# Seven half products in place of eight for w_out in some pair stages, sums of x kept in DRAM, half of each value tile copied on chip

## Chip, cores and metric

The kernel runs on one core of a Trainium2 chip. The metric is the device time of one execution in microseconds (us); lower is better. Engines: PE multiplies matrices, DVE and ACT (and POOL, GpSimd) work on elements, SP issues the DMA transfers.

## What is computed

The reference applies attention with a local window and 32 global tokens per sequence, then two feed-forward layers, all in fp32:

```
s_ll = where(|i - j| <= 32, q_l @ k_l.T * scale, -1e9)      # local rows: window
a_l  = softmax([q_l @ k_g.T * scale, s_ll]);  out_l = a_l @ [v_g, v_l]
out_g = softmax(q_g @ [k_g, k_l].T * scale) @ [v_g, v_l]     # 32 global rows
x = reshape(out, (2304, 512))                               # 4 sequences x 576 tokens
x = max(x @ w_in, 0)**2 @ w_out                             # moe:  512 -> 2048 -> 512
x = max(x @ w2_in, 0)**2 @ w2_out                           # moe2: the same shape
```

## The kernel before

Tokens stand in columns, features in partitions. The 2304 tokens are five blocks: block 0 (384 columns, with the global tokens), pair A (blocks 1 and 2, 512 columns each) and pair B (blocks 3 and 4, 384 each). Every fp32 operand is split into a high and a low part (`whi`, `wlo`; `xh`, `xl`; `gh`, `gl`), and a product is three passes on PE: high x high, high x low, low x high (L584 to L586).

Each layer has eight stages of 256 hidden features, that is two chunks of w_in and two of w_out (128 x 512 each, "weights"). The first stage of the first layer ("begin") runs among the attention, block by block. The other 15 run afterwards, each over block 0, pair A and pair B in the order that `CFG['order']` names. A weight arrives as 64-bit numbers in `wraw` (one buffer) by SP's queue, is turned into fp32 in `wt` by one ACT or DVE and four DVE instructions (L505 to L516) and split into a slot of `whi`/`wlo` (9 slots).

For w_in, a pair is multiplied by the scheme of Strassen and Winograd: seven half products instead of eight. It takes two weight slots with sums of the two chunks (`sums`, L530) and three sums of x per pair (`tsums`, L750), which are split once per layer and lie in SBUF (`tAh`, `tAl`, `tBh`, `tBl`). The half products collect in PSUM and in staging tiles `r` (L720). Then `activate` squares the positive part and splits it into `gh` and `gl`, and `second` multiplies by w_out: per block four output tiles `d`, each from two chunks, six passes. `finish` adds each into `y` (L642).

Attention works on 32 pairs of heads: keys and queries `kq`, values `v` (eight slots of 128 x 130: the window of each group of 32 queries, so most values come twice from DRAM), scores (L332), softmax, transposes (L355), values (L369), transposes back into x (L387). PE also runs warm-up matmuls on zeros (L805) wherever nothing else is ready.

Nothing is ordered by hand: `Plan` records all operations with priorities, costs and dependences, and `Plan.order` plays them in its own clock and writes the program in the order that results. On the chip each engine, SP's queue too, keeps to its order and waits where an operand is late.

Of the kernel before, what the change touches and what calls it, by code (L numbers as in the profile page):

```python
# [21 lines left out]
UNITS = 8  # L22
NI = UNITS * H
WIN = 224
KEYS = 128
VW = 2 * (D + 1)
KW = 384
# [9 lines left out]
CFG = {'warm': 32,  # L37
 'sg': 'A',
 'tl': 'D',
 'EARLY': 8,  # L40
 'ev': 'AAAA',
 'yc': 'ADAD',
 'wl': 'DD',
 'gl': 'D',
 'xh': 'AA',
 'glob': [13.66, 40.71, 52.94, 62.9],
 'w0': 0.0,
 'w1': 2.444332206519449,
 'halves': [1],
 'moe': [-728.245, 2019.27, 252.018, 414.177, 727.924, -1738.197],  # L50
 'step': [0.3996, 0.0017, 4.1427, 0.0632, 2.0927, 0.4659],
 'NK': 4,
 'wa': 'DADAAAA',
 'lid': -2.391,
 'lmk': -70.51,
 'lead': 6.47,
 'vlead': 1.531,
 'NM': 2,
 'NS': 5,
 'NV': 2,  # L60
 'NR': 9,
# [31 lines left out]
class Plan:  # L93
# [36 lines left out]
    def order(self):  # L130
# [8 lines left out]
        while len(done) < len(self.ops):  # L139
# [67 lines left out]
def pe_r(n, m=128):  # L207
    return max(n + 32.5, 2 * m + 6) / 2400
# [3 lines left out]
def kernel(ctx: ExitStack, tc: tile.TileContext, kl, vl, gk, gv, win, wout, msk, idn, out):  # L212
# [64 lines left out]
    kg = tiles(ap_, "kg", 2, [128, 1152 + S])  # L277
    gmx = ap_.tile([128, 2, 2], F32, name="gmx")
    gsm = ap_.tile([128, 2], F32, name="gsm")
    masks = ap_.tile([128, 3, KEYS], F32, name="masks")  # L280
    ident = ap_.tile([128, 128], F32, name="ident")
    warm = ap_.tile([128, 128], F32, name="warm")
    zeros = warm[:, 0:1].to_broadcast([128, 272])
    late_opened, tt_ = [], {}

    def open_late():
        if not late_opened:
# [11 lines left out]
    cnt = {"S": 0, "PT": 0, "O": 0, "h": 0, "Y": 0, "r": 0, "x": 0}  # L299
# [6 lines left out]
    def load(prio, out_, in_, nbytes, reads, writes):  # L306
        add("SP", 0.475, prio, lambda: nc.sync.dma_start(out=out_, in_=in_), reads, writes, tail=nbytes / 380e3)


    def pair(j, prio):  # L310
# [11 lines left out]
        load(prio - lead, kq[kb], kl[j], 327680, A, (K,))  # L322
        load(prio - CFG["vlead"], vt[vb], vl[j], 128 * 32 * VW, A, (V,))
        sk = [take("S", CFG["S"]) for _ in range(2)]

        def scores():
            for t in range(2):
                for g in range(4):
                    c, w = KW + 128 * t + 32 * g, 160 * t + 32 * g
                    for e in range(2):  # L330
                        r = slice(64 * e, 64 * e + 64)
                        nc.tensor.matmul(out=bank[sk[e]][32 * g:32 * g + 32, t * KEYS:(t + 1) * KEYS],  # L332
                                         lhsT=kq[kb][r, c:c + 32], rhs=kq[kb][r, w:w + KEYS], start=True, stop=True)

        add("PE", 0.503, P(), scores, A + (K,), tuple(sk), mode="S")
        for e in range(2):
            s = sk[e]
            for t in range(2):
                qt = (u % 2) * 2 + t
                mi = 0 if qt == 0 else (2 if qt == 3 else 1)  # L340
                k = 2 * e + t
                add("DVE", 0.21, P(), lambda t=t, mi=mi, k=k, s=s: nc.vector.tensor_tensor_reduce(
                    out=st[sb][:, k, :], in0=bank[s][:, t * KEYS:(t + 1) * KEYS], in1=masks[:, mi, :],
# [29 lines left out]
        add("PE", 0.5, P(), pv, A + every + (V,), (ok,), mode="V")  # L373
# [29 lines left out]
    def glob(bb, prio):  # L403
# [14 lines left out]
        for g in range(2):  # L418
            load(prio - 2.9 + 0.05 * g, V[g][:, 0:1280], gv[2 * bb + g], 655360, A, (GV[g],))
# [537 lines left out]
```

## Time and profile before

| | before |
|---|---|
| time, median of 3 runs | 833.05 us (832.01 to 834.45) |
| profiled execution: time, span | 832.85 us, 831.1 us |
| PE, DVE, ACT, POOL busy | 817.9, 675.5, 432.1, 0.2 us |
| mean granted PE clock | 0.999 |
| DMA, mean over the span | 92 GB/s |

The span reaches from the first to the last instruction; 1.75 us of the execution lie around it. Busy times count an engine's time once, also where instructions overlap.

### The profile page before, as it was taken

The numbers are of one execution on the slowest core, as the hardware profiler recorded it, in microseconds if no ns is written. First come the engines' busy times: TensorE is split into PE (matmuls) and PEld (weight loads), VectorE is DVE, ScalarE is ACT, GpSimd is POOL, SyncE is SP. The second block draws the span as 40 slices with busy tenths as digits, with TensorE's granted clock in tenths as the row PEclk, the third lists the DMA queues.
The fourth block names the chain that finished last, engine by engine and source line by source line (L and its number), as shares of the span: only waits on it lengthen the run. The fifth ranks groups of instructions, "written<-read, shape, count | busy, mean of one in ns | idle before, by whom it ended". The sixth has DMA issues, their size and how long they took to land.

```text
span 831.1 us, 16130 instructions
## 1 busy us (share of the span) xinstructions
PE 817.9 (98%) x6504; PEld 728.2 (88%) x6504; DVE 675.5 (81%) x1580; ACT 432.1 (52%) x934; POOL 0.2 (0%) x4
## 2 busy tenths in 40 slices
PE   9899999999999999999999999999999999999998
PEld 7676767899898998899898998899898989989997
DVE  4779788997887788878889998878887879688654
ACT  5886967653445334535356666535444444445341
POOL 0000000000000000000000000000000000000000
PEclk9999999999999999999999999999999999999999
DMA  9899874101111012102020111102020102020023
GB/s 348 309 371 315 307 244 171 50 2 51 52 52 51 26 54 74 51 26 73 30 76 1 34 52 68 51 26 77 26 77 26 55 22 77 26 77 26 26 76 140
DMA packets 23978, 76.79 MB, mean 92 GB/s; under 512 B 2656, under 2 KB 4448, under 8 KB 23904
## 3 DMA queue, kind: packets, MB, share of 16 engines
q1 hardware_dynamic: 23904, 75.77, 25.6%
q8 instruction: 51, 0.84, 0.4%
q14 instruction: 23, 0.19, 0.1%
HBM read 71.30 MB, written 4.46 MB: 91 GB/s over the span
## 4 chain that ended last, share of the span: by engine, by line
PE 91%; DMA 4%; DVE 3%; ACT 2%; issue 1%; ACTq 0%; DVEq 0%
PE O L585 7%; PE O L586 7%; PE O L584 7%; PE h L584 7%; PE h L586 7%; PE h L585 7%; PE S L586 6%; PE S L585 6%; PE S L584 6%; PE Y L584 4%; PE Y L586 4%; PE Y L585 4%; PE PT L586 4%; PE PT L584 4%; PE PT L585 4%; DMA v<-vl 2%
## 5 line engine op out<-in xcount | busy, mean ns | idle before, releaser
L243 DVE TENSOR_TENSOR gl<-r,gh 128x384 fp32r<-128x384 f32 (+2 forms) x162 | 97.5, 603 | 52.0 <-ACT r L613 43.5
L584 PE MATMUL O<-gh,whi 128*128 128x384 f32 (+1 forms) x304 | 108.2, 356 | 0.0
L586 PE MATMUL O<-gh,wlo 128*128 128x384 f32 (+1 forms) x304 | 108.2, 356 | 0.0
L585 PE MATMUL O<-gl,whi 128*128 128x384 f32 (+1 forms) x304 | 108.2, 356 | 0.0
L539 ACT ACTIVATE whi<-wt 128x512 fp32r<-128x512 f32 x94 | 58.7, 626 | 79.0 <-DVE wt L516 63.6
L642 DVE TENSOR_TENSOR y<-y,O 128x384 f32<-128x384 f32 (+1 forms) x140 | 82.0, 602 | 11.0 <-PE O L586 10.8
L584 PE MATMUL h<-xh,whi 128*128 128x384 f32 (+2 forms) x210 | 75.8, 361 | 0.0
L243 DVE TENSOR_TENSOR wlo<-wt,whi 128x512 fp32r<-128x512 f32 x94 | 64.4, 686 | 12.3 <-ACT whi L539 12.3
L585 PE MATMUL h<-xl,whi 128*128 128x384 f32 (+2 forms) x210 | 73.5, 350 | 0.7 <-DVE xl L399 0.7
L586 PE MATMUL h<-xh,wlo 128*128 128x384 f32 (+2 forms) x210 | 73.4, 350 | 0.0
L584 PE MATMUL Y<-gh,whi 128*128 128x384 f32 (+2 forms) x192 | 69.9, 364 | 0.5 <-DVE y L231 0.5
L585 PE MATMUL S<-xl,whi 128*128 128x384 f32 (+1 forms) x198 | 69.9, 353 | 0.0
L586 PE MATMUL S<-xh,wlo 128*128 128x384 f32 (+1 forms) x198 | 69.9, 353 | 0.0
L584 PE MATMUL S<-xh,whi 128*128 128x384 f32 (+1 forms) x198 | 69.7, 352 | 0.0
L586 PE MATMUL Y<-gh,wlo 128*128 128x384 f32 (+2 forms) x192 | 67.5, 352 | 0.1
L585 PE MATMUL Y<-gl,whi 128*128 128x384 f32 (+2 forms) x192 | 67.5, 351 | 0.0
L585 PEld LDWEIGHTS O<-gl,whi 128*128 128x128 f32 x304 | 57.1, 188 | 4.8
L586 PEld LDWEIGHTS O<-gh,wlo 128*128 128x128 f32 x304 | 57.1, 188 | 4.7
L584 PEld LDWEIGHTS O<-gh,whi 128*128 128x128 f32 x304 | 57.1, 188 | 4.7
L606 ACT ACTIVATE gh<-r 128x512 fp32r<-128x512 f32 (+1 forms) x60 | 34.7, 578 | 47.0 <-DVE r L604 46.9
L613 ACT ACTIVATE r<-r 128x384 f32<-128x384 f32 (+2 forms) x102 | 56.6, 555 | 3.1
L610 ACT ACTIVATE gh<-r 128x384 fp32r<-128x384 f32 (+2 forms) x102 | 56.0, 549 | 2.3 <-PE O L586 0.5
(125 smaller groups left out, 1846.6 us busy)
## 6 DMA issues: line engine op xcount, KB each, us to landing
v<-vl SPq DMA_DIRECT2D x32, 520.0 KB, 5.3
wraw<-win SPq DMA_DIRECT2D x32, 512.0 KB, 3.2
wraw<-wout SPq DMA_DIRECT2D x32, 512.0 KB, 3.3
kq<-kl SPq DMA_DIRECT2D x32, 320.0 KB, 5.5
y<-gv SPq DMA_DIRECT2D x8, 640.0 KB, 7.5
kg<-gk SPq DMA_DIRECT2D x8, 576.0 KB, 8.2
out<-y SPq DMA_DIRECT2D x12, 192.0 KB, 1.9
out<-y SPq DMA_DIRECT2D x8, 256.0 KB, 2.9
```

The source lines that it names most:

```text
L243: add("DVE", dve(n), prio, lambda: nc.vector.tensor_tensor(out=get(out_), in0=get(a), in1=get(b), op=ALU.subtract), reads, writes, lock=True)
L539: nc.scalar.activation(out=whi[slot], in_=tf, func=AF.Copy)
L584: nc.tensor.matmul(out=out_, lhsT=hi, rhs=xhi, start=start, stop=False, skip_group_check=again)
L585: nc.tensor.matmul(out=out_, lhsT=hi, rhs=xlo, start=False, stop=False, skip_group_check=again)
L586: nc.tensor.matmul(out=out_, lhsT=lo, rhs=xhi, start=False, stop=stop, skip_group_check=again)
L606: add("Activation", act(nb) + 0.04, P(), lambda: nc.scalar.activation(out=a, in_=r, func=AF.Copy), (R,), GH)
L610: add("Activation", act(nb) + 0.04, P(), lambda: nc.scalar.activation(out=a, in_=r, func=AF.Square), (R,), GH)
L613: add("Activation", act(nb) + 0.04, P(), lambda: nc.scalar.activation(out=r, in_=r, func=AF.Square), (), (R,))
L642: add("DVE", dve(nb), P(), lambda: nc.vector.tensor_tensor(out=yd, in0=yd, in1=o, op=ALU.add), (yk[d],), (Y,))
```

## The change

Three parts, and a new table of numbers (`CFG`) that sets priorities, buffers and engines.

1. **w_out in seven half products.** `CFG['so']` names the pairs of each stage that use it. `back` multiplies there seven half products of two output tiles, with two more weight slots that hold sums of the w_out chunks, and with differences of the squared activations (`mix`, L904), in place of the two calls of `second`. Each half product belongs to one or two places of `y` and is added there (`deliver`, L697), so there are 12 or 14 additions per pair in place of 8. Squares stay in `r` and are split by `op`.
2. **Sums of x in DRAM.** They are written to `saved` when they are made and read back before each pair's products into a ring of six tiles `tr`.
3. **Half of the value tiles copied on chip.** DMA brings four of the eight slots, POOL copies the rest.

The table changes, among others: 11 weight slots, 13 staging tiles, 3 value tiles, 4 slots in place of 8 before the attention's memory is free, 11 warm-up matmuls, one low part of a weight in four on POOL (`wl`), squares on ACT (`gs`) but one in four (`gf`), evictions on ACT.

```diff
-CFG = {'warm': 32,
+CFG = {'warm': 11,
...
+ 'EARLY': 4,
+ 'vc': 'PP',
+ 'ev': 'A',
+ 'yc': 'A',
+ 'wl': 'DPDD',
...
- 'NR': 9,
+ 'NV': 3,
+ 'NR': 13,
...
+ 'NSLOT': 11,
+ 'NG': 4,
+ 'NTR': 6,
...
+ 'tm': 'RRRR',
+ 'so': ['', 'AB', 'A', 'A', 'AB', '', '', 'A', 'AB', 'A', 'AB', 'B', 'AB', 'AB', 'A'],
+ 'wp': [-242.15, -537.45],
...
+ 'gf': 'ADAA',
+ 'gs': 'A',
...
+    drm = ctx.enter_context(tc.tile_pool(name="drm", bufs=1, space=bass.MemoryType.DRAM))
+    saved = {(g, n, i): drm.tile([128, 2, NB[b]], F32, name=f"td{g}{n}{i}")
+             for g, (b, _) in PAIRS.items() for n in (2, 3, 4) for i in range(2)}
...
-            for g, (b, _) in PAIRS.items():
-                for n in (2, 3, 4):
-                    tt_[g, n] = [lp.tile([128, 2, NB[b]], F32R, name=f"t{g}{k}{n}") for k in "hl"]
...
+            for j in range(NTR):
+                tring.append(lp.tile([128, 2, 512], F32R, name=f"tr{j}"))
...
-        load(prio - lead, kq[kb], kl[j], 327680, A, (K,))
-        load(prio - CFG["vlead"], vt[vb], vl[j], 128 * 32 * VW, A, (V,))
+        load(prio - lead, kq[kb], kl[j], 512 * (KW + 256), A, (K,))
+        load(prio - CFG["vlead"], vt[vb][:, 0:4 * VW], vl[j], 128 * 16 * VW, A, (V, ("v2", vb)))
+        for p0, n, to, src in ((0, 128, 4, 0), (0, 32, 4, 1), (0, 64, 6, 1), (64, 64, 6, 0)):
+            rows = slice(p0, p0 + n)
+            copy("vc", prio - CFG["vlead"] + 1e-3, vt[vb][rows, to * VW:(to + 2) * VW], vt[vb][rows, src * VW:(src + 2) * VW],
+                 2 * VW, A + (V,), (("v2", vb),))
...
-                (half(t0, 1), half(t0, 1), half(t1, 1), ALU.subtract, (T1,), T0)):
+                (half(t0, 1), half(t0, 1), half(t1, 1), ALU.subtract, (T1,), T0)) if kind == "in" else (
+                (half(t1, 1), half(t0, 1), half(t1, 1), ALU.add, (T0,), T1),
+                (half(t0, 1), half(t0, 0), half(t0, 1), ALU.subtract, (), T0),
+                (half(t0, 0), half(t1, 1), half(t0, 0), ALU.subtract, (T1,), T0),
+                (half(t1, 0), half(t1, 0), half(t0, 0), ALU.subtract, (T0,), T1))):
...
+            add("DVE", dve(nb), P(), lambda: nc.vector.tensor_tensor(out=yd, in0=yd, in1=o, op=ALU.add), (k,), (Y,))
...
+        activate(P, f, nb, hp, hk, half)
...
+        def t(n):
+            got = []
+            for i in range(2):
+                if (g, n, i) in direct:
+                    r, R = direct.pop((g, n, i))
+                else:
+                    r, R = granule()
+                    lr, lw = late_keys(R)
+
...
+                    load(P(), dst, saved[g, n, i], 1024 * nb, (("td", g, n, i, 0), ("td", g, n, i, 1)) + lr, (R,) + lw)
+                got.append((lambda r=r: tring[r][:, 0, 0:nb], lambda r=r: tring[r][:, 1, 0:nb], R))
...
+        if fork:
+            copy("sf", P(), A, B, nb, (kb,), (ka,), psum=True)
+        else:
+            keep(0)
+        product(kc, C, sa, 0, x(b1, 0), True)
         product(kb, B, sa, 2, t(2), False)
         keep(1)
...
+        product(ka, A, f0, 2, x(b0, 2), not fork)
+        if fork:
+            square(P, nb, A, ka, s[0], G[0])
+        else:
+            plus(0, ka, A)
+            square(P, nb, s[0], G[0], s[0], G[0])
...
+        add("Activation", act(nb) + 0.04, P(), hi, (R,) + lr, GH + lw)
+        minus("gl", P(), l, r, lambda: a().bitcast(F32), nb, (R,) + GH, GL)
+        return f
...
+    def back(W, g, P, sG, stages):
...
+        (r11, r12, r22, r21), (R11, R12, R22, R21) = sG
+        (o0, o1), (p1, p0) = W["out"], W["osum"]
+        banks = [take("Y", CFG["Y"] + CFG["PT"] + CFG["O"]) for _ in range(4)]
...
+        def product(two, slot, h, X, start, ys):
+            a, l, K = X
+            for d in range(2):
+                o = bank[two[d]][:, 0:nb]
+                add("PE", c3, P(), lambda o=o, d=d: three(
+                    o, wv(whi, slot)[:, 2 * h + d, :], wv(wlo, slot)[:, 2 * h + d, :], a(), l(), start, True, not start),
+                    (("w", slot),) + K, (two[d],))
+                for b, k in ys:
+                    n = seen[b, k + d] = seen.get((b, k + d), 0) + 1
+                    last = 1 if (b, k) == (b0, 2) or (forked and (b, k) == (b0, 0)) else 2
+                    deliver(P, b, k + d, two[d], stages, None, stages[1] and n == 1, stages[2] and n == last)
...
+        X, K = banks[0:2], banks[2:4]
+        B21, B11 = opd(r21, R21), opd(r11, R11)
+        forked = pick("sx") == "A" and min(wide.get(k, 0) for k in X) >= nb
...
+        if forked:
+            product(K, o0, 0, B11, True, ())
+            for d in range(2):
+                add("Activation", act(nb), P(), lambda d=d: nc.scalar.activation(
+                    out=bank[X[d]][:, 0:nb], in_=bank[K[d]][:, 0:nb], func=AF.Copy), (K[d],), (X[d],))
+            product(X, o1, 0, B21, False, ((b0, 0),))
+        else:
+            product(X, o1, 0, B21, True, ((b0, 0),))
+            product(K, o0, 0, B11, True, ((b0, 0),))
+        mix(r12, r12, r11, (R11,), R12)
+        product(X, p1, 1, opd(r12, R12), True, ((b1, 2),))
+        B22 = opd(r22, R22)
+        mix(r22, r22, r12, (R12,), R22)
+        product(K, p0, 0, opd(r22, R22), False, ((b1, 0),))
+        product(X, p1, 0, B22, False, ((b1, 0),))
+        mix(r11, r22, r11, (R22,), R11)
+        product(K, p0, 1, opd(r11, R11), False, ((b1, 2),))
+        mix(r21, r21, r22, (R22,), R21)
+        product(K, o1, 1, opd(r21, R21), False, ((b0, 2),))
...
+            if n == 1:
+                hi_, lo_, K = lambda: xh[b1][:, i, :], lambda: xl[b1][:, i, :], (("x", b1, i),) * 2
+            elif ring:
+                r, R = granule()
+                direct[g, n, i] = r, R
+                lr, lw = late_keys(R)
+                hi_, lo_, K = lambda: tring[r][:, 0, 0:nb], lambda: tring[r][:, 1, 0:nb], (R, R)
+            else:
+                (v, V), (w, X) = staging(), staging()
+                hi_, lo_, K = lambda: v[:, 0:nb].bitcast(F32R), lambda: w[:, 0:nb].bitcast(F32R), (V, X)
...
+            if n > 1:
+                for e, f in enumerate((hi_, lo_)):
+                    load(P(), saved[g, n, i][:, e, :], lambda f=f: f().bitcast(F32), 512 * nb, (K[e],), (("td", g, n, i, e),))
```

PE, in the second stage after the attention, w_out on 512 columns (`Y`, `PT`, `O` are PSUM banks; equal names with other numbers are other buffers). Before, at the end of pair A: each bank gets two chunks (slots 105/113 and 100/108).

```order
L584 MATMUL PT_147<-gh_79,whi_105 128x512
L585 MATMUL PT_147<-gl_83,whi_105 128x512
L586 MATMUL PT_147<-gh_79,wlo_113 128x512
L584 MATMUL PT_147<-gh_80,whi_100 128x512
L585 MATMUL PT_147<-gl_84,whi_100 128x512
L586 MATMUL PT_147<-gh_80,wlo_108 128x512
L584 MATMUL O_148<-gh_79,whi_105 128x512
L585 MATMUL O_148<-gl_83,whi_105 128x512
L586 MATMUL O_148<-gh_79,wlo_113 128x512
L584 MATMUL O_148<-gh_80,whi_100 128x512
L585 MATMUL O_148<-gl_84,whi_100 128x512
L586 MATMUL O_148<-gh_80,wlo_108 128x512
```

Now, in the middle of pair A: slot 2756/2757 and slot 2750/2751 hold sums of the two w_out chunks; half products go to two banks each.

```order
L636 MATMUL Y_163<-gh_80,whi_2756 128x512
L637 MATMUL Y_163<-gl_84,whi_2756 128x512
L638 MATMUL Y_163<-gh_80,wlo_2757 128x512
L636 MATMUL PT_166<-gh_80,whi_2756 128x512
L637 MATMUL PT_166<-gl_84,whi_2756 128x512
L638 MATMUL PT_166<-gh_80,wlo_2757 128x512
L636 MATMUL O_167<-gh_82,whi_2750 128x512
L637 MATMUL O_167<-gl_86,whi_2750 128x512
L638 MATMUL O_167<-gh_82,wlo_2751 128x512
L636 MATMUL O_168<-gh_82,whi_2750 128x512
L637 MATMUL O_168<-gl_86,whi_2750 128x512
L638 MATMUL O_168<-gh_82,wlo_2751 128x512
```

What moved: sixteen bank visits of three passes for a pair become fourteen, and the visits wait for the differences of the activations in turn.

DVE, the same stage, pair B. Before: half products into `r`, squares (L604), low parts (`gl`), with a weight's steps among them.

```order
L720 TENSOR_TENSOR r_92<-r_92,S_146 128x384
L512 TENSOR_SCALAR wt_97<-wt_97 128x512
L604 SCALAR_TENSOR_TENSOR r_92<-r_92 128x384
L514 SCALAR_TENSOR_TENSOR wt_97<-wraw_96,wt_97 128x512
L243 TENSOR_TENSOR gl_84<-r_92,gh_80 128x384
L516 SCALAR_TENSOR_TENSOR wt_97<-wraw_96,wt_97 128x512
L720 TENSOR_TENSOR r_91<-r_91,S_146 128x384
L243 TENSOR_TENSOR gl_86<-r_93,gh_82 128x384
L604 SCALAR_TENSOR_TENSOR r_91<-r_91 128x384
L243 TENSOR_TENSOR wlo_114<-wt_97,whi_106 128x512
L243 TENSOR_TENSOR gl_83<-r_91,gh_79 128x384
L642 TENSOR_TENSOR y_77<-y_77,Y_144 128x384
```

Now: no squares on DVE here, the differences (L904) and additions into y between them.

```order
L264 TENSOR_TENSOR wlo_2761<-wt_102,whi_2760 128x512
L264 TENSOR_TENSOR gl_86<-r_94,gh_82 128x384
L820 TENSOR_TENSOR r_95<-r_95,S_164 128x384
L264 TENSOR_TENSOR gl_84<-r_96,gh_80 128x384
L264 TENSOR_TENSOR gl_85<-r_97,gh_81 128x384
L904 TENSOR_TENSOR r_95<-r_95,r_94 128x384
L904 TENSOR_TENSOR r_96<-r_96,r_95 128x384
L904 TENSOR_TENSOR r_94<-r_96,r_94 128x384
L697 TENSOR_TENSOR y_77<-y_77,Y_163 128x384
L697 TENSOR_TENSOR y_77<-y_77,PT_166 128x384
L264 TENSOR_TENSOR gl_83<-r_95,gh_79 128x384
L264 TENSOR_TENSOR gl_85<-r_96,gh_81 128x384
```

What moved: differences, their low parts and the additions into `y` stand in one chain with the next half products.

SP's queue, some stages later. Before, it holds only weights:

```order
L307 DMA wraw_96<-win 128x1024
L307 DMA wraw_96<-wout 128x1024 x2
L307 DMA wraw_96<-win 128x1024 x2
L307 DMA wraw_96<-wout 128x1024 x2
L307 DMA wraw_96<-win 128x1024 x2
L307 DMA wraw_96<-wout 128x1024 x2
```

Now the reads of sums (`tdA`, `tdB`) stand among the weights:

```order
L348 DMA tr_2769<-tdA_154 128x1024
L348 DMA tr_2764<-tdA_149 128x1024
L348 DMA wraw_100<-win 128x1024
L348 DMA tr_2765<-tdA_150 128x1024
L348 DMA tr_2766<-tdA_151 128x1024
L348 DMA wraw_100<-wout 128x1024
L348 DMA tr_2767<-tdA_152 128x1024
L348 DMA tr_2768<-tdA_153 128x1024
L348 DMA wraw_100<-wout 128x1024
L348 DMA tr_2769<-tdA_154 128x1024
L348 DMA tr_2764<-tdB_155 128x2x384
L348 DMA wraw_100<-win 128x1024
```

What moved: a read behind a weight in this queue is issued only after that weight, which waits for its one buffer.

## Rows read from the trace of the kernel before

**Rows 1.** Page, engines: busy us, share of the span, instructions.

```profile
PE 817.9 (98%) x6504; PEld 728.2 (88%) x6504; DVE 675.5 (81%) x1580; ACT 432.1 (52%) x934; POOL 0.2 (0%) x4
```

**Rows 2.** Windows: length, busy us per engine, granted clock, DMA share, GB/s.

```profile
0.00:20.00 20.00, 18.48 (x313) 15.89 (x314) 9.59 (x54) 9.73 (x28) 0.20 (x4) 1.00 0.92 346
20.00:80.00 60.00, 55.59 (x1376) 41.37 (x1374) 48.38 (x243) 48.66 (x153) 0.00 (x0) 1.00 0.93 335
80.00:140.00 60.00, 57.35 (x1241) 43.39 (x1234) 48.44 (x218) 45.04 (x137) 0.00 (x0) 1.00 0.74 265
140.00:160.00 20.00, 18.89 (x172) 16.43 (x171) 18.44 (x35) 11.96 (x26) 0.00 (x0) 1.00 0.08 27
160.00:820.00 660.00, 660.00 (x3376) 604.24 (x3375) 547.23 (x1028) 313.57 (x591) 0.00 (x0) 1.00 0.14 49
```

**Rows 3.** Timeline of PE: start us, length us, line, operation.

```profile
199.92 0.33 PE L584 MATMUL O<-gh,whi 128*128 128x384 f32 x1
...
204.95 0.33 PE L586 MATMUL O<-gh,wlo 128*128 128x384 f32 x1
205.12 0.39 PE L584 MATMUL h<-xh,whi 128*128 128x512 f32 x1
...
209.69 0.39 PE L586 MATMUL h<-tAh,wlo 128*128 128x512 f32 x1
```

**Rows 4.** Timeline of DVE, instructions that follow without a wait.

```profile
223.44 0.43 DVE L530 TENSOR_TENSOR wt<-wt,wt 128x256 f32<-128x256 f32 x1
223.78 0.68 DVE L642 TENSOR_TENSOR y<-y,O 128x512 f32<-128x512 f32 x1
...
239.96 0.43 DVE L512 TENSOR_SCALAR wt<-wt 128x512 uint32<-128x512 uint32 x1
240.31 0.55 DVE L642 TENSOR_TENSOR y<-y,PT 128x384 f32<-128x384 f32 x1
240.77 0.69 DVE L514 SCALAR_TENSOR_TENSOR wt<-wraw,wt 128x512 uint32<-128x512 uint32 x1
241.37 0.55 DVE L642 TENSOR_TENSOR y<-y,O 128x384 f32<-128x384 f32 x1
241.84 0.69 DVE L516 SCALAR_TENSOR_TENSOR wt<-wraw,wt 128x512 uint32<-128x512 uint32 x1
```

**Rows 5.** Groups by form, ACT: count, busy us, mean ns, idle before.

```profile
L613 ACT ACTIVATE r<-r 128x512 f32<-128x512 f32 x32 | 20.2, 632 | 0.9
```

**Rows 6.** Chain that ended last, its value loads: start us, us.

```profile
62.12 4.87 DMA v<-vl
...
78.76 6.09 DMA v<-vl
...
96.64 8.92 DMA v<-vl
```

**Rows 7.** Page, DMA issues: count, KB each, median us to landing.

```profile
v<-vl SPq DMA_DIRECT2D x32, 520.0 KB, 5.3
wraw<-win SPq DMA_DIRECT2D x32, 512.0 KB, 3.2
...
kq<-kl SPq DMA_DIRECT2D x32, 320.0 KB, 5.5
```

**Rows 8.** PE's longest wait; the group of warm-up matmuls.

```profile
PE O L369 <- DMA v<-vl: 3.1, 3, 1.6
...
L805 PE MATMUL O<-warm 128*128 128x128 f32 x64 | 11.7, 336 | 1.5 <-DVE warm L803 1.0 <-ACT xh L228 0.5
```

**Rows 9.** Waits of SP's queue: us in total, times, longest us.

```profile
SPq L307 <- DVE wt L516: 563.3, 56, 31.7
```

More of the change, by code (lines that the diff above doesn't have):

```diff
@@ L149, in order @@
             op = heapq.heappop(avail[e])[2]
+            if e == "DVE" and op.lock and port.get("Pool", 0.0) > t:
+                rest = [x for x in avail[e] if not x[2].lock]
+                if rest:
+                    other = min(rest)
+                    avail[e].remove(other)
+                    heapq.heapify(avail[e])
+                    heapq.heappush(avail[e], (op.prio, op.seq, op))
+                    op = other[2]
             if op.lock or e == "Pool":
@@ L306, in load, with window @@
     def load(prio, out_, in_, nbytes, reads, writes):
-        add("SP", 0.475, prio, lambda: nc.sync.dma_start(out=out_, in_=in_), reads, writes, tail=nbytes / 380e3)
+        get = lambda v: v() if callable(v) else v
+        add("SP", 0.475, prio, lambda: nc.sync.dma_start(out=get(out_), in_=get(in_)), reads, writes, tail=nbytes / 355e3)
+    def window(a, G):
+        p = [32 * POS[G + (i - G) % 3] for i in range(3)]
+        return bass.AP(tensor=a.tensor, offset=a.offset + p[0], ap=[a.ap[0], [p[2] - p[0], 2], [p[1] - p[0], 2], [1, 32]])
     def pair(j, prio):
@@ L741, in tsums @@
+    direct = {}
+    def tsums(g, prio, from_y, ring, step=1e-3):
         b0, b1 = PAIRS[g]
@@ L832 @@
                 continue
-            W = weights((KF * layer + 2 * p, KF * layer + 2 * p + 1), 1000, 0, True)
+            both = (KF * layer + 2 * p, KF * layer + 2 * p + 1)
+            W = {}
+            W["in"], W["sum"] = weights("in", both, 100 * (stage + 1) + CFG["wp"][0], 0, True)
             if stage == 0:
                 for i, g in enumerate(PAIRS):
-                    tsums(g, CFG["tp"][i], False)
+                    if CFG["tm"][i] == "S" or CFG["order"][0][0] != g:
+                        tsums(g, CFG["tp"][i], False, False)
             order = CFG["order"][stage]
@@ L857, with pending @@
                     pending()
-                if rest:
-                    theirs = [turn % NGT, (turn + 1) % NGT]
-                    turn += 2
-                    rest(P, theirs)
-                    second(P, blocks[0], mine, W["out"], True, True, stages)
-                    mine = theirs
-                def pending(P=P, b=blocks[-1], mine=mine, W=W, stages=stages, free=n == len(order) - 1, j=j, stage=stage):
-                    second(P, b, mine, W["out"], True, True, stages)
+                if n == 0:
+                    W["out"], W["osum"] = weights("out", both, 100 * (stage + 1) + CFG["wp"][1], 0, CFG["so"][stage] != "")
+                def pending(P=P, mine=mine, W=W, stages=stages, free=n == len(order) - 1, j=j, stage=stage, pairs=pairs):
+                    if j == "0":
+                        second(P, 0, [op(P, NB[0], *v) for v in mine], W["out"], True, True, stages)
+                    else:
+                        (back if j in CFG["so"][stage] else plain)(W, j, P, mine, stages)
+                        if j == pairs[-1]:
+                            release(*W["osum"])
                     if free:
                         release(*W["out"])
-                    if stages[0] == 0 and stages[2] and j != "0":
-                        tsums(j, 100 * (stage + 1) + CFG["tp"][2 + "AB".index(j)], True)
             stage += 1
```

401 lines of the change are left out of this document (243 added, 158 removed).

## Prediction

> **What bounds the kernel now.** I read the page's engine shares first. PE is busy 817.9 us of 831.1, DVE 675.5, ACT 432.1, and POOL does nothing [rows 1]. A mean hides stages, so the next view is the table of stretches [rows 2]: from 160 to 820 us PE is busy 660.00 of 660 us, DVE 547 (83%), ACT 314 (48%), the DMA engines 14%. Before 160 us it is another kernel: the DMA engines are 92 and 93% busy up to 80 us and 74% after it, and PE lacks 1.52, 4.41, 2.65 and 1.11 us, 9.7 us together. "Busy" for PE does not yet mean at its best rate, so the third view is PE's timeline [rows 3]: 29 passes of 384 columns in a row start 5.03 us apart, 0.1735 us each, and 20 of 512 columns 4.57 us, 0.2285 each. One matmul stage has 48 passes on block 0, 90 on pair A (512 columns) and 90 on pair B (384): 8.3 + 20.6 + 15.6 = 44.5 us. Fifteen stages make 667 us, which is what the trace has room for. So from 160 us on PE runs without a gap, and only fewer passes can shorten that part; before it PE waits for tiles that DMA brings, and fills gaps with warm-up matmuls.
>
> **The change, part by part.**
>
> *Fewer passes.* The table names 11 pairs A and 7 pairs B for the seven products (18; the title says 17). Each such pair makes 42 passes for w_out in place of 48; the order of PE shows the four sum-built products. 11 x 6 x 0.2285 + 7 x 6 x 0.1735 = 15.1 + 7.3 = **22.3 us** off an engine without gaps. A gain unless another engine now keeps PE waiting.
>
> *DVE.* This decides. Its durations are taken start to start where nothing waits [rows 4]: 0.60 us for a two-input instruction on 512 columns, 0.47 on 384, 0.34 on 256, 0.35 for a one-input one on 512. The instruction list of DVE grows by 97 of 512 columns, 36 of 384 and 45 of 256, and loses 19 one-input ones: 58.2 + 16.9 + 15.3 - 6.7 = 84 us more, so 675 + 84 = 759 us of about 805. By stage, now: four weights 7.5 + 0.4, six low parts 3.6, sums for w_in 1.4, block 0 2.8, pair A 17 x 0.60 = 10.2, pair B 17 x 0.47 = 8.0: 33.9 of 44.5 us (76%). After: weights 7.5, low parts 3.6 (six of eight; the other two go to POOL), both sums 2.7, block 0 3.1. A pair with eight products costs some 15 instructions (A 9.0, B 6.8): two of the three squares that DVE made go to ACT. A pair with seven costs four differences and four to six additions into y more: A about 24.5 (14.7 us), B, whose start is copied by ACT, 22.5 (10.6 us). Stages with both pairs: 42.2 us of DVE against 44.5 - 2.4 = 42.0 of PE. Stages with A alone 38.4 against 43.1; with none 30.4 against 44.5. Over 15 stages 573 against 644 us (89%), plus some 25 us at the change of layers, which falls beside the stages 5 and 6 without any. So DVE is full in six stages, but each has a neighbour with 5 to 14 us to spare, except stages 12 and 13.
>
> *POOL.* 30 low parts of weights move to it, of which the trace has no row, only memsets [rows 1]. Bounds: nothing, where an addition from PSUM runs on DVE meanwhile; above, two runs over the operands at DVE's 0.69 us [rows 4], 1.4 us, in which DVE does nothing. Two each in the six full stages, on top of the 0.2 us by which these are over: 6 x (0.2 + 2.8) = 18 us; elsewhere the slack takes them. Nothing excludes either end. I take **4 us**, nearer to nothing: 368 additions into y and 71 into half products take one operand from PSUM and can stand there (some 230 us of them in all), and the order mixes them with the weights' steps. The Trainium skill (SBUF — State Buffer, "Who interferes with whom") says that a DVE instruction with two SBUF inputs contends with a GpSimd one that reads SBUF, and whoever starts first keeps the shared pair of ports for the whole instruction. By that rule alone the term would be 18 and the sum 822; no run so far shows it.
>
> *ACT.* 236 more instructions at 0.63 us at most [rows 5]: 432 + 149 = 581 of 805 us, 72%. At nothing: its slack covers it; were an operand late by one such instruction in each of 18 pairs it would cost 11 us, inside the bound above.
>
> *Sums of x through DRAM.* 162 reads of 512 or 384 KB (74 MB) and 48 writes join SP's queue. From 160 to 820 us the DMA engines move 49 GB/s at 14% [rows 2]; 80 MB more in 640 us makes 174 GB/s, 50%. A tile of 512 KB lands 3.2 us after its issue [rows 7], and between the sum products of one pair and of the next PE has 42 to 58 passes, 8 to 12 us. Six tiles of 512 KB take 9.4 us at the 335 GB/s of 20 to 80 us, each started when its tile is free: just in time. Cost nothing; if that cover is gone, up to 3.2 us for each of the 27 groups of six.
>
> *Attention.* 32 value tiles shrink from 520 to 260 KB, keys grow by 32 KB: about 8 MB less of the 43 MB moved by 145 us, 24 us of transfer at 335 GB/s. The chain of waits runs through value loads for 4.9, 6.1 and 8.9 us [rows 6], but PE stood still for them only 3.1 us [rows 8], since it had other work in those times. What PE can get back is its 9.7 us and the warm-up matmuls beyond the first 5 us, in which no key tile has landed (5.5 us from issue to landing [rows 7]): 11.7 - 5 = 6.7 us [rows 8], together 16. It can lose too: without fillers the first 20 us hold 18.5 - 11.7 = 6.8 us of PE work, which at 1.2 GHz, the lower level, would cost 7 more; the granted clock of that stretch is 1.00 (2.4 GHz), but with the fillers in it. The four copies of a tile on POOL (0.34 us each on DVE's scale, 1.4 together) stand between landing and use; the third value buffer gives one pair's time, 140/32 = 4.4 us, so they are hidden. Between -16 and +7 I take **-6**: about a third of the most, because the gaps before 20 us come from dependences that no smaller tile shortens, while DMA ceases to be the limit after that.
>
> *Sum.* From the profiled execution's 832.85 us (0.2 below the median of 833.05): 832.85 - 22.3 + 4 - 6 = 808.5, I say **808 us**.
>
> **The rivals.**
>
> *DVE and POOL take the bound (0.23).* For it: 42.2 against 42.0 us in six stages, and PSUM banks that are freed only by DVE. Against: PE never waits for DVE now at 76%, and slack lies beside. Time: 832.85 - 22.3 - 6 + 18 = 822 (816 to 830). This is where the Trainium skill's rule on the shared ports (above) would lead.
>
> *Everything is hidden and attention gets nearly all back (0.09).* For it: 660 of 660 now. 832.85 - 22.3 - 14 = 796 (793 to 800).
>
> *Slower: SP's queue (0.07).* Raw weights have one buffer, and SP already stands 563 us before it, waiting for DVE's last use, 56 times, up to 31.7 us [rows 9]. A read of sums behind such a load starts only when DVE, now full, has let go. From 24/27 = 0.9 us of lateness per group of six on, the whole gain is gone; with a full landing in every second group 13.5 x 3.2 = 43 us: about 852. Against it: in the list reads stand in runs of up to six between two weights, and the weights are converted stages ahead (11 slots).
>
> *No change (0.04).* Needs 24 us of these waits by chance; that passes are not on the path is excluded by [rows 2].
>
> **How the numbers follow.** The likeliest (0.57): PE stays the bound, 800 to 816, 808. The range takes in four fifths of the DVE rival (0.18) and of the hidden one (0.07), so 794 to 826 holds 0.82; its ends are near the bounds of the two unknown terms (832.85 - 22.3 - 16 = 794.5, and 822 with half of attention's 6 lost). A change under 0.3% (2.5 us) cannot be told from none here. Faster: 0.57 + 0.22 + 0.09 = 0.88; same 0.05 with the DVE rival's last edge; slower 0.07.
>
> **What would show it.** Right: PE busy without gaps between about 150 and the end, 108 passes fewer, DVE near 95% there, POOL some 40 us in that part, no row of PE waiting for a tile of sums. The DVE step is wrong if the table of waits has PE behind additions into y or behind low parts for more than 10 us in the stages with both pairs, or if DVE's two-input instructions last longer while POOL works. The SP step is wrong if PE waits for loads of sums. The attention step: PE's missing time before 160 us, 9.7 us now, should fall below 7, and DMA's share in 20 to 80 us below 85%; a granted clock under 1.00 in the first 20 us would show the loss. What would make the whole wrong is an in-order queue that slips once and takes two others with it; then waits of several us stand on PE's timeline, not fractions.

## The result, and the profile after

The change made the kernel 1.4% slower: 844.91 us median (842.76 to 845.21), ratio to the kernel before 1.0137 (95% interval 1.0114 to 1.0159), where 808 (794 to 826) was predicted. The profiled execution took 842.76 us, 9.9 more than before's.

Below: the page's engine line of the changed kernel and its chain (the work that ended last, followed back from the end), then the chain of the kernel before, then the windows of the changed kernel (columns as in [rows 2]).

```profile
PE 806.3 (96%) x6354; PEld 703.5 (84%) x6354; DVE 753.5 (90%) x1739; ACT 544.3 (65%) x1170; POOL 98.8 (12%) x162
...
PE 54%; DVE 31%; ACT 6%; DMA 6%; issue 3%; POOL 0%; ACTq 0%; SPq 0%; DVEq 0%
```

```profile
PE 91%; DMA 4%; DVE 3%; ACT 2%; issue 1%; ACTq 0%; DVEq 0%
```

```profile
0.00:20.00 20.00, 16.03 (x269) 10.80 (x269) 10.02 (x53) 9.62 (x26) 4.15 (x14) 1.00 0.93 345
20.00:80.00 60.00, 56.10 (x1385) 41.27 (x1386) 46.85 (x235) 48.48 (x150) 30.70 (x68) 1.00 0.82 280
80.00:140.00 60.00, 58.29 (x1307) 44.82 (x1306) 40.45 (x204) 47.76 (x146) 22.96 (x52) 1.00 0.55 179
145.00:178.00 33.00, 23.69 (x106) 18.68 (x105) 32.70 (x60) 20.67 (x42) 1.67 (x1) 0.90 0.53 180
178.00:830.00 652.00, 639.83 (x3226) 576.08 (x3225) 613.12 (x1173) 412.43 (x798) 37.88 (x27) 1.00 0.51 170
```

DVE is as full as forecast (753.5 against 759 us). But the chain, 91% PE before, is now 54% PE and 31% DVE, and for its length the stretch of 145 to 178 us, where the first stage after the attention begins, has lost most. The kernel before has there:

```profile
145.00:178.00 33.00, 32.31 (x169) 29.30 (x168) 32.21 (x64) 20.48 (x41) 0.00 (x0) 1.00 0.10 33
```

63 passes fewer in the same 33 us. PE's longest waits from 145 us on (total us, times, longest) follow:

```profile
PE S L636 <- ACT xh L976: 5.0, 1, 5.0
PE O L637 <- DVE gl L264: 2.7, 4, 1.3
PE Y L637 <- DVE gl L264: 2.7, 5, 1.4
PE Y L636 <- ACT y L249: 2.2, 3, 1.1
PE O L636 <- ACT gh L873: 1.7, 1, 1.7
PE S L636 <- DVE r L820: 1.6, 2, 0.8
```

**The balance.** I took each pass from PE's timeline with the pitch of [rows 3] (from one pass's start to the next where nothing waits: 0.1735 or 0.2285 us) and called what stands beyond it lost. That includes pauses too short for the rows of waits and passes at a lower clock. After 150 us PE makes 3342 passes, before 3460: the 108 that were to go and 10 that attention has got ahead by (78 fewer of 512 columns, 40 fewer of 384). That is 24.8 us of passes less. Lost are 14.0 us between 150 and 200 us (before 1.5) and 23.4 us after it (before 1.3): 34.6 more. -24.8 + 34.6 = +9.8; measured +9.9.

**The wait of 5 us.** PE's timeline (start, length), then ACT's, then the window behind the wait:

```profile
167.77 0.34 PE L638 MATMUL h<-xh,wlo 128*128 128x384 f32 x1
173.10 0.79 PE L636 MATMUL S<-xh,whi 128*128 128x512 f32 x1 [4.99 <-ACT xh L976]
...
174.84 0.63 PE L636 MATMUL h<-tr,whi 128*128 128x512 f32 x1
175.27 0.63 PE L637 MATMUL h<-tr,whi 128*128 128x512 f32 x1
175.69 0.63 PE L638 MATMUL h<-tr,wlo 128*128 128x512 f32 x1
```

```profile
169.64 0.63 ACT L976 ACTIVATE tr<-r 128x512 fp32r<-128x512 f32 x1
171.48 0.67 ACT L558 ACTIVATE wt<-wraw 128x512 f32<-128x512 f32 x1 [1.21 <-DMA wraw<-win]
172.05 0.47 ACT L856 ACTIVATE r<-S 128x384 f32<-128x384 f32 x1
172.42 0.62 ACT L976 ACTIVATE xh<-r 128x512 fp32r<-128x512 f32 x1
```

```profile
173.00:177.00 4.00, 3.66 (x7) 2.13 (x7) 3.92 (x7) 1.62 (x4) 0.00 (x0) 0.50 0.73 245
```

ACT stands 1.21 us before the first step of a weight that has not landed, with `xh` behind it. After the wait passes of 512 columns stand 0.43 us apart in place of 0.2285: from 173 to 177 us the granted clock is 0.50, that is 1.2 GHz. So this wait is paid a second time, with some 2 us.

**Late in the stages.** A piece of the chain of waits of the changed kernel (start, us, what):

```profile
657.91 0.60 DVE r L904
658.51 0.34 DVE wt L584
658.84 0.60 DVE r L904
659.45 0.34 DVE wt L584
659.78 0.61 DVE gl L264
660.39 0.04 issue
660.44 0.50 PE O L637
```

DVE runs back to back; the low part that PE needs at once (`gl`) stands behind four sums of weights (`wt`) that this product does not read: its first pass, with the same weights, had already started at 659.23. Such losses are small and many: after 200 us PE's longest wait is 1.7 us.

### The profile page after: what moved, and what is told of

Read it like the earlier page. It is cut to its first block, busy times and chain, and to the rows that moved or that the text cites. A ratio compares the mean times of both kernels' runs of the same rounds, so it can differ in the third digit from the quotient of the medians.

```text
span 841.0 us, 17085 instructions
## 1 busy us (share of the span) xinstructions
PE 806.3 (96%) x6354; PEld 703.5 (84%) x6354; DVE 753.5 (90%) x1739; ACT 544.3 (65%) x1170; POOL 98.8 (12%) x162
## 4 chain that ended last, share of the span: by engine, by line
PE 54%; DVE 31%; ACT 6%; DMA 6%; issue 3%; POOL 0%; ACTq 0%; SPq 0%; DVEq 0%
DVE y L697 8%; PE h L636 5%; DVE gl L264 5%; PE h L638 4%; PE h L637 4%; PE O L636 4%; PE O L637 4%; PE O L638 4%; DMA wraw<-win 4%; PE S L636 3%; PE S L638 3%; PE S L637 3%; PE Y L636 2%; PE Y L637 2%; DVE wlo L264 2%
## 5 line engine op out<-in xcount | busy, mean ns | idle before, releaser
L873 ACT ACTIVATE gh<-r 128x384 fp32r<-128x384 f32 (+1 forms) x204 | 114.3, 568 | 52.6 <-PE O L638 29.6
L264 DVE TENSOR_TENSOR gl<-r,gh 128x384 fp32r<-128x384 f32 (+2 forms) x216 | 133.1, 628 | 4.3 <-ACT gh L873 2.8
L593 ACT ACTIVATE whi<-wt 128x512 fp32r<-128x512 f32 x118 | 73.9, 627 | 70.2 <-DVE wt L566 28.8
L697 DVE TENSOR_TENSOR y<-y,O 128x512 f32<-128x512 f32 (+1 forms) x192 | 114.5, 612 | 5.4 <-PE O L638 5.3
L267 POOL TENSOR_TENSOR wlo<-wt,whi 128x512 fp32r<-128x512 f32 x30 | 42.2, 1408 | 631.7 <-ACT whi L593 450.4
L861 ACT ACTIVATE r<-r 128x384 f32<-128x384 f32 (+1 forms) x130 | 73.0, 564 | 1.8
L636 PE MATMUL Y<-gh,whi 128*128 128x384 f32 (+2 forms) x174 | 64.5, 371 | 4.8 <-ACT y L249 2.6
L257 POOL TENSOR_SCALAR v<-v 64x260 f32<-64x260 f32 (+2 forms) x128 | 56.4, 448 | 75.9 <-DMA v<-vl 28.9
L637 PE MATMUL Y<-gl,whi 128*128 128x384 f32 (+2 forms) x174 | 61.8, 355 | 2.7 <-DVE gl L264 2.7
L558 ACT ACTIVATE wt<-wraw 128x512 f32<-128x512 f32 x64 | 42.7, 667 | 28.7 <-DMA wraw<-win 19.0
```

The lines of the kernel that those rows point to most:

```text
L257: add("Pool", 0.16 + 0.00085 * n + (0.08 if key == "nm" else 0.0), prio, lambda: nc.gpsimd.tensor_scalar(out=out_, in0=in_, scalar1=1.0 if ...
L264: add("DVE", dve(n), prio, lambda: nc.vector.tensor_tensor(out=get(out_), in0=get(a), in1=get(b), op=ALU.subtract), reads, writes, lock=True)
L267: add("Pool", 0.25 + 0.0021 * n, prio, lambda: nc.gpsimd.tensor_tensor(out=get(out_), in0=get(a), in1=get(b), op=ALU.subtract), reads, writes)
L558: add("Activation", act(512) + 0.04, P(), lambda: nc.scalar.activation(out=tf, in_=high.bitcast(F32), func=AF.Abs), (R,), (T,))
L593: nc.scalar.activation(out=whi[slot], in_=tf, func=AF.Copy)
L636: nc.tensor.matmul(out=out_, lhsT=hi, rhs=xhi, start=start, stop=False, skip_group_check=again)
```

## Experiments

Lost time is worked out as above, for the one profiled execution; times are medians of several, and ratios compare with executions of the kernel before in the same session. Executions of one kernel differ by 6 us and more (834.3 to 840.7 in thin_raw), so a difference of 2 or 3 us between two lost times says little. Kernels of the first table keep the changed kernel's order of instructions; only the size of some is cut, so that their results are incomplete (in pool_on_dve the engine of some is changed, and the result is whole).

| kernel | time, ratio to before (95%) | lost 150-200 | lost after 200 |
|---|---|---|---|
| changed | 844.9, 1.0137 (1.0114-1.0159) | 14.0 | 23.4 |
| thin_mix | 840.0, 1.0068 (1.0041-1.0095) | 14.3 | 19.4 |
| pool_on_dve | 853.6, 1.0244 (1.0193-1.0294) | 14.8 | 33.0 |
| thin_reads | 839.1, 1.0073 (1.0046-1.0099) | 14.7 | 18.4 |
| thin_tsums | 843.7, 1.0128 (1.0082-1.0173) | 12.2 | 28.0 |
| thin_raw | 836.8, 1.0023 (0.9998-1.0047) | 14.3 | 21.7 |
| thin_weights | 834.1, 0.9993 (0.9971-1.0016) | 12.6 | 14.8 |
| thin_act | 845.5, 1.0148 (1.0119-1.0178) | 14.3 | 23.1 |
| thin_start | 830.4, 0.9965 (0.9944-0.9985) | 10.2 | 16.2 |
| thin_all | 823.4, 0.9885 (0.9853-0.9917) | 9.6 | 9.8 |

**thin_mix**

```diff
-    out=out_, in0=a, in1=b, op=op_          # mix
+    out=out_[:, 0:8], in0=a[:, 0:8], in1=b[:, 0:8], op=op_
```

> Same order of instructions as the changed kernel; the 72 differences of the squared activations (L904) and the 44 of 48 or so sums of w_out chunks work on 8 columns in place of 512, 384 or 256, so these parts of the result are left out. DVE loses 44 x 0.53 + 28 x 0.40 + 44 x 0.27 = 46 us of work. Theory D (DVE is full from 180 us on and PE waits for it): of the 23 us by which PE's passes stand apart more than before after 178 us, most go: 824 to 832 us. Theory P (DVE is late only where GpSimd holds it): 839 to 845. Theory T (only the 13 us lost at 150 to 178 us matter): 842 to 845, the loss there unchanged.

The sums of w_out chunks are cut in the same way. DVE's busy time fell by 37 us (753.5 to 716.6; 46 were expected), which bought some 5. Theory D has its direction, not its size: for most of PE's lost time the differences are not what it stands behind. The time lies in theory P's range; the next run speaks against P.

**pool_on_dve**

```diff
-    nc.gpsimd.tensor_tensor(out=get(out_), in0=get(a), in1=get(b), ...   # minus, wlo
+    nc.vector.tensor_tensor(out=get(out_), in0=get(a), in1=get(b), ...
```

> Same order; the 30 low parts of weights that POOL made are made by DVE at the same place of the program (0.60 us each, 18 us more DVE work; GpSimd keeps the value copies). Theory P (GpSimd's 1.4 us instructions hold DVE's two-input ones, some 9 us of waiting seen in the rows): the holds go and PE gains, 834 to 842 us. Theory D (DVE is full, every added us of DVE costs): 18 - 9 = 9 us more work, 845 to 855. Theory T: 844 to 848.

Slower by some 9 us, as theory D has it, and not faster, as P had it. GpSimd's low parts are a gain, in spite of the waiting they cause (last section).

**thin_reads** and **thin_tsums**

```diff
-    return tring[r][:, :, 0:nb].bitcast(F32)         # and the same of saved
+    return tring[r][:, :, 0:32].bitcast(F32)
```

```diff
+    m = nb if from_y or out_ is not a else 8         # tsums: out_, a, b [:, 0:m]
```

> Same order; the 162 reads of sums of x bring 32 columns in place of 512 or 384, so most of the operand is stale and that part of the result is left out; the transfers fall from 74 MB to 5 MB, the issues stay. Theories D, P and T: no change, 842 to 847 us. Theory S (the reads, or DMA traffic that slows weights behind them, are late): 825 to 838.

> Same order; 16 of the 32 DVE instructions that make the sums of x at the start of the first layer (L958, those in place) work on 8 columns, so these sums are left out; DVE loses 8 x 0.53 + 8 x 0.40 = 7.4 us of work at 140 to 180 us, where it is 99% busy. Theory T (DVE's backlog there delays stage 0, PE stands 5 us for xh and its clock falls): the stall of 5 us goes and 8 to 13 us come back, 832 to 838. Theory D with slack further on (a late start is caught up, or later stalls take its place): 841 to 845.

The reads cost 5 us, though no row has PE waiting for one; the time lies between the theories' ranges. The raw weights carry this. Their time from issue to landing, in the stretch from 200 to 840 us, is as follows (changed kernel, then thin_reads):

```profile
DMA to landing us min/median/max: 3.3/3.6/6.6
```

```profile
DMA to landing us min/median/max: 3.4/3.6/4.4
```

So some weights come late beside the reads, and ACT's waits for raw weights in that stretch are 19.2 us, with short reads 12.8.

The sums, of which half were cut, are no cause by themselves: the 5 us wait stayed 5.0. The 28.0 us after 200 us are from an execution 2.4 us above the median.

**thin_raw** and **thin_weights**

```diff
+    m = 1024 if conv[0] == 1 else 64
-    load(P(), wraw[rb]...("p c t -> p (c t)"), src.bitcast(U32), ...
+    load(P(), wraw[rb]...("p c t -> p (c t)")[:, 0:m], src.bitcast(U32)[:, 0:m], ...
```

```diff
-    out=t, in0=high, scalar=0xC0000000, in1=t, ...   # and L560, L562, L566
+    out=t[:, 0:8], in0=high[:, 0:8], scalar=0xC0000000, in1=t[:, 0:8], ...
```

> Same order as the changed kernel; from the second weight on, a raw weight is brought with 64 of its 1024 numbers per row, so the weights' values are stale and that part of the result is left out; its landing time falls from 3.6 us to some 2. Theory W (one raw buffer: last use by DVE, load, ACT's L558, DVE's four steps follow one another, 8 us per weight, and with four early slots in place of eight the first stage's weights are made after 145 us in place of before, ACT standing behind the load with xh queued behind it): the 5 us stall and most of the 13 us lost at 150 to 178 us go, 832 to 838. Theory D (DVE full everywhere): 841 to 846.

> Same order; the four DVE steps that turn a raw weight into fp32 (L560 to L566) work on 8 of 512 columns, so the weights' values are wrong; DVE loses 60 x (2 x 0.28 + 2 x 0.53) = 97 us of work, spread over all stages, and each weight's chain gets 1.6 us shorter. Theory D: PE's stalls after 178 us (20 us more than before) nearly all go, and those at 150 to 178 us in part: 808 to 822. Theory W: only the 13 us at 150 to 178 us go: 830 to 836. If what PE waits for is neither, 838 to 845.

By their ratios times fell by 9 and 12 us (thin_raw's profiled execution took 840.7, above its median, so its lost time shows less of it). Both times lie in theory W's ranges, but by luck: the wait for `xh` stays 4.6 and 5.3 us, and the loss of 150 to 200 us stays 14.3 and 12.6. What came back in thin_weights lay after 200 us (23.4 to 14.8), as theory D has it, though not nearly all of it.

**thin_act** takes 8 columns in L854, L861 and, from the fifth on, L873; **thin_start** joins raw, tsums and weights; **thin_all** joins these with mix, reads and act.

> Same order as the changed kernel; ACT's second steps of the squares (L854, L861) and, from the fifth on, the copies into gh (L873) work on 8 columns in place of 512 or 384, so that part of the result is left out: some 400 instructions by 0.4 us, about 150 us less of ACT's 544. Theory A (ACT, with 65% busy, is itself late: squares, copies and raw weights in one order, each waiting in turn): PE's stalls after 178 us go by half or more, 826 to 835 us. Theory D (DVE alone is late; ACT's slack is real): 841 to 846.

> The edits of thin_raw, thin_tsums and thin_weights together, same order. Theory of a tie (at 150 to 178 us two chains end within a microsecond of each other, DVE's sums of x and ACT behind a raw weight that lands, so that taking one alone gives nothing): the 5 us stall and the half clock after it go, and the 13 us lost there fall below 6; whole 820 to 829. Rival (the order itself makes PE wait there, for evictions and memory that comes free at 145 us): 13 us stay, 830 to 835 as with thin_weights alone.

> All of thin_mix, thin_reads, thin_raw, thin_tsums, thin_weights and thin_act together, same order; the products of PE, the additions into y, the low parts and the evictions stay. Theory D with A (all of PE's stalls are lateness of DVE, ACT and loads; the 108 passes are really saved): PE without gaps, 808 to 816 us. If PE's passes are stretched by something else, or the order of PE's own queue holds it: 820 to 832.

ACT's busy time fell from 544 to some 415 us and nothing changed: its load is no bound. At the start even three cuts together (thin_start) leave 4.0 us of the wait, and 830.4 us is the lower edge of the rival's range. With the load alone cut (thin_raw) ACT stands 0.85 us before `xh` for a sum of DVE; with all three cut it runs back to back up to `xh`. So DVE, the load and ACT end there close together, as the theory of a tie has it, but breaking the tie gives back only 3.8 of 14.0 us. Windows of thin_all:

```profile
145.00:178.00 33.00, 27.14 (x121) 22.18 (x120) 25.02 (x66) 22.19 (x48) 2.59 (x2) 0.95 0.41 138
178.00:820.00 642.00, 636.24 (x3241) 579.83 (x3239) 497.61 (x1173) 273.39 (x791) 34.94 (x26) 1.00 0.11 27
```

With all of it gone, 18.0 of the 37.4 us lost came back and 19.4 remain, and the time reaches 823, not 808: the rival of that expectation. Of the 19.4, 9.6 lie at the start and 3.5 in the first stage of the second layer (stages counted back from the last pass by their numbers of passes). That stage loses 3.5 to 4.1 us in every kernel of this table.

The second table's kernels change the table or the planner, so the order is laid anew in all but none_thin, which keeps that of so_none.

| kernel | time, ratio to before (95%) | passes after 150 us | lost 150-200 | lost after 200 |
|---|---|---|---|---|
| before | | 3460 | 1.5 | 1.3 |
| so_none | 859.3, 1.0283 (1.0246-1.0320) | 3463 | 14.3 | 16.4 |
| none_thin | 850.8, 1.0207 (1.0170-1.0245) | 3446 | 14.0 | 8.2 |
| again | 857.5, 1.0279 (1.0242-1.0316) | 3381 | 16.5 | 25.6 |
| costs | 853.8, 1.0226 (1.0203-1.0250) | 3340 | 13.1 | 35.8 |
| b_early4 | 843.6, 1.0116 (1.0077-1.0154) | 3475 | 9.8 | 1.1 |
| b_wa | 839.4, 1.0074 (1.0047-1.0100) | 3479 | 3.3 | 0.8 |
| b_costs | 849.3, 1.0189 (1.0150-1.0229) | 3492 | 4.7 | 6.8 |

**so_none** (`'so': [''] * 15`) and **none_thin** (so_none with the edits of thin_raw and thin_reads)

> No stage uses seven half products for w_out; sums of x in DRAM, value copies and the rest of the table stay, and the program is ordered anew. PE gets 22.3 us of passes back, DVE loses the differences, sums and additions, some 110 us. Theory D (the seven products cost what they give, through DVE): without them the stalls after 178 us go too, 845 + 22 - 20 = 847, 842 to 852. Theory W (the loss sits where the layers begin, and the seven products paid): 845 + 22 = 867, 860 to 870. If the seven products cost more than they give: below 840.

> The kernel so_none in its order, with raw weights of 64 numbers per row and reads of 32 columns as in thin_raw and thin_reads, so that part of the result is left out. Theory S (the transfers, one raw buffer and the reads before it in one queue, make ACT and then PE late): most of the 17 us that so_none loses after 178 us go, 840 to 848. Rival (the order and the engines, not the transfers): 852 to 860.

Nearest to theory W: without the seven products the kernel is slower still, by 1.0283 - 1.0137 = 0.0146 of 834, 12 us. So between these two orders they earn 12 of their 22, and what came with them costs 24 (0.0283); how much of either is the new order alone is not separated. Its passes after 150 us are before's: attention has gained nothing there. The loss is where theory W has it, 14.3 us at the start and 6.5 of the 16.4 after 200 us in the first stage of the second layer. And it comes without DVE being full: from 300 to 400 us DVE is 72% busy, and ACT makes PE late there (ACT's timeline of so_none, then PE's):

```profile
316.92 0.62 ACT L873 ACTIVATE gh<-r 128x512 fp32r<-128x512 f32 x1
320.48 0.66 ACT L558 ACTIVATE wt<-wraw 128x512 f32<-128x512 f32 x1 [2.94 <-DMA wraw<-wout]
321.04 0.62 ACT L861 ACTIVATE r<-r 128x512 f32<-128x512 f32 x1
321.56 0.48 ACT L249 ACTIVATE h<-S 128x384 f32<-128x384 f32 x1
```

```profile
322.09 0.44 PE L636 MATMUL S<-tr,whi 128*128 128x384 f32 x1 [1.62 <-ACT h L249]
```

ACT stands 2.94 us for a weight that has not landed, and PE 1.62 us for the eviction behind it. Short transfers (none_thin) halve what is lost after 200 us (8.2, of which 6.1 in the first stage of the second layer) and bring some 6 us, between theory S and its rival; the 14 us at the start they leave.

**again** (raised durations of the planner, its table set again, 10 pairs A and 5 B) and **costs** (raised durations alone: `1.045` to `1.073`, `0.835` to `0.902`, `n + 33` to `n + 36`)

> The changed kernel with its order laid out anew: the planner's durations raised towards the traces (DVE by 2.7%, ACT by 8%, a pass by 3 columns, GpSimd's additions to 1.48 us), and its table set again under them, with seven half products in 10 pairs A and 5 pairs B (18.9 us of passes less than before) and the weights of each stage made earlier against its products. Theory L (what PE waits for is an order laid for a clock that the engines do not keep; DVE and ACT have room enough if the order leaves it where they run late): at the start of the layer below 5 us lost, after it below 12, and faster than the kernel before: 816 to 830. Rival (DVE at 90% is too full for any order with these parts): 836 to 846.

> The changed kernel with the planner's raised durations alone, its table as it was, so that the program is ordered anew. Theory L: better than the changed kernel by some us, 834 to 842. Rival (the table, set for the old durations, no longer fits and the order gets worse at random): 845 to 862, as with the eight products everywhere.

Both misses for theory L: the order laid for slower engines lost more, not less. The kernel costs lies in its rival's range, the kernel again above its rival's too.

**b_early4** (`'EARLY': 4` in the kernel before), **b_wa** (`'wa': 'A'`) and **b_costs** (raised durations)

> The kernel before with 4 weight slots in place of 8 until the attention's memory is free, and nothing else; the order is laid anew with it. Theory E (the 13 us lost at 145 to 178 us come from the first stage's weights that can only be made after 145 us): 842 to 850, with PE's loss in that stretch, and few gaps after it. Rival: 830 to 837, no loss there; then the sums of x or the order lose it.

> The kernel before with ACT alone making the first step of each weight (before: 5 of 7), and nothing else; the order is laid anew with it. Theory H (ACT stands behind a raw weight's load and what is queued behind it makes PE wait): 838 to 848. Rival (harmless while loads come early): 830 to 837.

> The kernel before with the planner's durations raised (DVE 2.7%, ACT 8%, a pass by 3.5 columns) and nothing else, so that its order is laid anew. Theory R (an order that fits badly costs only where DVE and ACT are near full; at DVE 76% of a stage the slack takes it): 830 to 838 us, PE without gaps after 180 us. Rival N (any order that its table was not set for costs tens of us, whatever the load): 845 to 870.

b_early4 is as theory E has it. Four early slots lose 8.3 us more than before between 150 and 200 us and nothing later; its order is new as well:

```profile
145.00:178.00 33.00, 27.36 (x118) 24.36 (x119) 28.19 (x55) 15.98 (x34) 0.00 (x0) 0.84 0.09 32
178.00:830.00 652.00, 651.97 (x3329) 596.09 (x3328) 541.85 (x1018) 308.64 (x581) 0.00 (x0) 1.00 0.15 50
```

b_wa's time lies in theory H's range, but mostly not by its mechanism. Of its 5 us 3.3 are 19 passes more left at 150 us and 1.8 are lost before 200 us; after that PE loses 0.8, less than before. ACT's waits for raw weights from 200 to 840 us (b_wa, then the kernel before; us in total, times, longest):

```profile
ACT wt L508 <- DMA wraw<-win: 20.2, 11, 3.0
ACT wt L508 <- DMA wraw<-wout: 16.1, 12, 2.6
```

```profile
ACT wt L508 <- DMA wraw<-win: 11.1, 7, 3.3
ACT wt L508 <- DMA wraw<-wout: 10.2, 7, 3.3
```

ACT stands 36.3 us there, before 21.3, and PE hardly notices either. In the changed kernel it is 19.2 and in so_none 58.0. So ACT standing for a weight is not enough to hold PE; it matters what stands behind it and how soon PE needs that.

b_costs warns how far a new order's time goes: it alone cost 15 us, as its rival N had it. In the profiled execution, 16.3 us longer than before's, some 8 are in attention (32 passes of the layers and 81 small ones of attention more left at 150 us), 3 at the start and 6 in the first stage of the second layer. In the other stages all three orders kept PE without gaps, which no order of the changed kernel did.

## Why the prediction was wrong, point by point

- **Fewer passes: right.** 108 are gone, 22.4 us by the pitch (15.1 + 7.3; the prediction writes 22.3, and the title it speaks of names no number of pairs).
- **Waits of PE in the stages: the step that failed.** The sum had one term for them, 4 us with GpSimd (0 to 18), on the ground that "DVE is full in six stages, but each has a neighbour with 5 to 14 us to spare"; ACT and the sums of x stood at nothing. Measured are 34.6 us beyond before's, 12.5 of them up to 200 us (next point) and 22.1 after. DVE's total was right; that slack nearby covers the rest was wrong. By stages (counted as above) the six with both pairs lost 8.4 us and the other eight after the first 14.8, although those were to have the slack: DVE is 92 to 100% busy in twelve of the fourteen. What PE needs next stands behind work for others in a queue that keeps its order (the piece of the chain above), and the slack of the next stage comes after PE has waited. Cuts on DVE give back up to 8.6 of the 22.1 us (thin_weights), shorter reads 5.0, all cuts 13.6. A full DVE is not the whole cause: so_none loses 16.4 us after 200 us with DVE at 72%.
- **The signs.** DVE near 95% (613 of 652 us), GpSimd 38 us, 108 passes fewer and no row of PE waiting for sums all came, and the forecast was still wrong. The sign against the DVE step, over 10 us of PE behind additions or low parts in stages with both pairs, did not come: the rows of these waits make 7.4 us over all stages. PE without gaps was the one sign that told.
- **The first stage: left out.** The sum had no term for 145 to 178 us, where [rows 2] show DVE at 18.44 of 20 us already. 12.5 us were lost between 150 and 200 us. The table's 4 early slots in place of 8 were named and never priced: the kernel before has split eight weights by 100 us and goes on at 145, the changed one has split four by 53 us and the next from 139 us on (ACT's L539 and L593). b_early4 puts 8.3 us on that in the kernel before, but without the 5 us wait for `xh`; how much of the 12.5 it is here stays open, since the changed kernel was not run with eight.
- **GpSimd:** the mechanism is there, some 7 us of DVE's time, but in nine of 30 cases; moving the work back costs 9 us.
- **ACT at nothing:** right for its load (thin_act), wrong for its place: 5.0, 2.2 and 1.7 us of PE's longest waits end with ACT.
- **Sums of x at nothing, and SP's queue:** no row of PE waiting for reads, as said; but the transfers cost 5 (thin_reads) to 9 us (thin_raw). The rival had late transfers right and what is late wrong: not reads behind weights, but weights beside reads, up to 6.6 us to landing in place of 4.4.
- **Attention:** -6 taken, -2 got (10 passes), and none in so_none. Its last pass starts 5.7 us earlier (138.9 us, before 144.6), but fewer passes of the layers were done beside it. PE's missing time before 160 us was to fall under 7 us; it is 3.97 + 3.90 + 1.71 and 2.35 in 140 to 160, 11.9. DMA's share in 20 to 80 us fell below 0.85 as forecast, and the granted clock of the first 20 us stayed 1.00.
- The prediction's last sentence, an in-order queue that slips and takes others with it in waits of several us, is what happened at the start, once (5.0 us). After 200 us it is fractions.

What stays open: the 19.4 us that thin_all still loses, above all the start and the first stage of the second layer, and why attention gains so little. No version here that computes the whole result beats the kernel before.

## What to carry to other kernels

Count slack where it is used: for each result that the bound engine waits for, what stands before it in its queue, and whether that is needed then. A step that waits for a transfer can hold up an engine's urgent work behind it (so_none), and costs nothing where nothing urgent stands behind it (b_wa after 200 us): the order decides, not the engine's load. In a program whose order a planner lays, a newly laid order alone moved the time by 15 us, more than half of the 24 us that the change was to bring; such a change is judged against a few orders of the old kernel, and cuts that keep the order tell causes apart best.

## What the runs showed of the hardware

GpSimd's subtraction of 128 x 512 takes 1.41 us, twice DVE's 0.69. Timeline of the changed kernel, GpSimd and DVE at two places:

```profile
534.36 1.33 POOL L267 TENSOR_TENSOR wlo<-wt,whi 128x512 fp32r<-128x512 f32 x1 [19.92 <-ACT whi L593]
```

```profile
534.47 1.78 DVE L264 TENSOR_TENSOR gl<-r,gh 128x512 fp32r<-128x512 f32 x1
```

```profile
283.64 1.29 POOL L267 TENSOR_TENSOR wlo<-wt,whi 128x512 fp32r<-128x512 f32 x1 [18.79 <-PE O L638]
```

```profile
283.69 0.55 DVE L697 TENSOR_TENSOR y<-y,Y 128x384 f32<-128x384 f32 x1
284.15 0.55 DVE L697 TENSOR_TENSOR y<-y,PT 128x384 f32<-128x384 f32 x1
```

The DVE instruction that reads two SBUF tiles lasts 1.78 us in place of 0.68 and ends 0.56 us after GpSimd's; additions that take one operand from PSUM run beside it at 0.55, as without it [rows 4]. The Trainium skill (SBUF — State Buffer, "Who interferes with whom") says that a DVE instruction with two SBUF inputs contends with a GpSimd one that reads SBUF, and that one with at most one SBUF input does not; the trace agrees. Such meetings were nine among 30, some 7 us together.
